# GpSimd takes over the section, relays the half sums and clears the tiles; x is loaded after the first weights; one load for A's output weights

## The chip, the cores and the metric

The kernel runs on one core of a Trainium2 chip. The core has TensorE (PE, matrix products into the accumulation memory PSUM), VectorE (DVE), ScalarE (ACT), GpSimd (POOL) and SyncE (SP), which here issues nearly all DMA transfers. The engines run by themselves and are tied together by semaphores. The metric is the device time of one execution in microseconds (us), and the median over executions is compared.

## What is computed

Two independent decode steps of attention, A and B, each for one query token, 32 heads with 128 elements each, and a cache of 16384 keys; their outputs stand side by side:

```
q = (x @ wq).reshape(1, 1, 32, 128)
scores = einsum("bhqd,bhkd->bhqk", q, k) * 128 ** -0.5
o = einsum("bhqk,bhkd->bhqd", softmax(scores), v)
out = o.reshape(1, 1, 4096) @ wo
return concatenate([a, b], axis=-1)
```

A reads all 16384 keys and values of every head, B only the last 4096. x has 512 elements, wq is 512x4096 and wo 4096x512, all in bf16. Every key, value and weight is used once, so the work is to bring 352 MB into the core and to do little with each byte.

## The kernel before

The program is written out by hand, one function for each engine; no scheduler changes the order. Inside one section (`tc.tile_critical`, L498) the five engines run freely. The section has an owner, `sync_engine=SP`: at the entry all engines wait for a signal of the owner, and at the end the owner gathers the others.

**Loads.** A is worked in 16 loads of two heads, B in 4 loads of eight heads; each is 8 MB of keys and 8 MB of values (`loads`, `st.R` heads at a time, for B in two halves `u`). SP (`_sync_program`, L126 and on) issues, all on one hardware queue: the query weights of A and of B (4 MB each, L132, into the tile `vt`), keys of load 0, then in turn keys of load i and values of load i-1 (L150), and at the end the output weights, cut into pieces (L171): A's in two of 2 MB, B's in five of 2, 1, 0.5, 0.25 and 0.25 MB. Keys have two buffers (`kt`), values one (`vt`). SP waits before keys of load i until the reduction of load i-2 is done (`s_red`), before values of load i-1 until the product with the values of load i-2 is done (`s_pv`), and before keys of load 1 until the query of A and B is projected (`s_q`). The pieces of the output weights wait for the product of the last load but one.

**Start.** GpSimd writes ones and makes from them an identity and a placement matrix (L180 to L189). ScalarE issues the loads of the two x rows (L199, 1 KB each) before anything else. VectorE clears what has to be zero: the tiles for the spread x (`xb_flat`), the selection tiles `sel`, two accumulators, and a 64-column strip `zero` (L245 to L249), and then makes masks and offsets out of the identity (L253 to L264). TensorE turns x into columns (`xT`), VectorE copies them spread out into `xb` (L271), and TensorE multiplies with the query weights when they are there: 32 matmuls of 512 columns for A, 32 for B.

**A load.** VectorE multiplies keys with the query (`mult`, L292) and adds the upper half of the 128 products to the lower half (`add`, L300). TensorE adds up the 64 half sums to 8 by matmuls with the identity (`red`). VectorE adds the last 8 (`scores`, L306), ScalarE takes the exponential (L216), TensorE multiplies with the values (`pv`), and VectorE picks the diagonal (`pick`, L320 to L327), which TensorE sums into the tile `f`. `add` is what releases `red`, by the semaphore `s_add`, which counts four quarters of a load (`NB` = 4). Load 0 is worked in four parts and load 1 in two, so that their adds post one or two quarters each. VectorE's order in load i is `mult(i)`, `scores(i-1)`, `add(i)`, `pick(i-1)`.

**End.** After the last load TensorE turns B's result into columns `oc` (`norm`) and takes the pieces of the output weights in order (`cx.pieces`, L514 and on): 32 matmuls of 512 columns for A, then 64 of 256 columns for B in groups of 32, 16, 8, 4 and 4. Each piece waits for its own semaphore. Every matmul is recorded at L364 (`mm`), so the tiles tell them apart: `red<-vt,ocA` and `red<-vt,ocB` are the output products. VectorE and ScalarE copy the rows out of PSUM and SP stores them (L174).

Of the kernel before, what the change touches and what calls it, by code (L numbers as in the profile page):

```python
# [19 lines left out]
KEYS = 256  # L20
NB = 4
# [153 lines left out]
    cx.s_end.wait(e, 32)  # L175


def _pool_program(nc, cx):
    e = nc.gpsimd
    e.memset(cx.one[:, :], 1.0)  # L180
    e.memset(cx.ones_col[:, :], 1.0)
    cx.s_own.on(e.memset(cx.ones, 1.0))
    cx.s_own.wait(e, 1)
    cx.s_pool.on(e.affine_select(
        out=cx.ident[:, :], in_=cx.ones[:, 0:P], pattern=[[-1, P]], compare_op=ALU.is_equal,
        fill=0.0, base=0, channel_multiplier=1,
    ))
    w = cx.place_at + 2 * P
    cx.s_pool.on(e.affine_select(  # L189
        out=cx.place[:, :], in_=cx.ones[0 : 2 * H, 0:w], pattern=[[1, w]], compare_op=ALU.is_equal,  # L190
        fill=0.0, base=-cx.place_at, channel_multiplier=-cx.n_r,
    ))


def _scalar_program(nc, cx, loads):
    e = nc.scalar
    stA, stB = cx.sts
    for w, st in enumerate(cx.sts):
        st.s_x.on(e.dma_start(out=cx.row[0:1, w * st.D : (w + 1) * st.D], in_=st.x[0, 0:1, :]), 16)  # L199
    n = 0  # L200
    for st in cx.sts:
        m = st.N // st.R // 512
        n += m
        cx.s_q.wait(e, n)
        st.s_qall.on(e.copy(st.qall[:, :], cx.red[:, 0:m, :].rearrange("p j f -> p (j f)")))
    cx.s_dve.wait(e, cx.n_off)
    for i, st in enumerate(loads):
        if i == stA.L:
            _orow(e, cx, stA)
        cx.s_sc.wait(e, i + 1)  # L210
        j = i if st is stA else i - stA.L
        for u in range(st.U):
            p = _p_view(cx, st, u)
            for g in range(st.R):
                h = st.f_at + (j * st.U + u) * st.R + g
                ins = e.activation(  # L216
                    out=p[:, :, g, :],
                    in_=cx.sc[:, u * st.keys : (u + 1) * st.keys].rearrange("p (t e) -> p t e", e=4),
                    func=ACT.Exp, scale=SCALE, bias=st.off[:, g : g + 1], accum_out=cx.cs[:, h : h + 1],
                )  # L220
            cx.s_p.on(ins)
    _orow(e, cx, stB)
    w = stB.DN // 2
    stB.s_o.wait(e, 1)
    stB.s_row.on(e.copy(cx.row[0:1, stB.at + w : stB.at + 2 * w], cx.out_ps(stB)[1]))
# [10 lines left out]
def _vector_program(nc, cx, loads):  # L236
    e = nc.vector
    stA, stB = cx.sts
    own = cx.s_dve

    def did(ins):
        return own.on(ins)

    for st in cx.sts:
        did(e.memset(st.xb_flat, 0.0))  # L245
        did(e.memset(st.sel[:, :], 0.0))
    for acc in cx.acc:
        cx.n_acc = did(e.memset(acc[:, :], 0.0))
    n = did(e.memset(cx.zero, 0.0))  # L249
    cx.n_zero = n  # L250
    cx.s_pool.wait(e, 1)
    ident = cx.ident[:, :]
    n = did(e.tensor_reduce(out=cx.rows, in_=ident.rearrange("p (c w) -> p w c", w=H), axis=AX.X, op=ALU.add))  # L253
    own.wait(e, n)
    for st in cx.sts:
        rows = cx.rows[:, 0 : 4 * st.R].rearrange("p (g e) -> p g e", e=4)
        did(e.tensor_reduce(out=st.mask[:, :], in_=rows.rearrange("p g e -> p e g"), axis=AX.X, op=ALU.add))
        did(e.tensor_reduce(out=st.sel[:, st.sel_at : st.sel_at + st.R], in_=rows, axis=AX.X, op=ALU.add))
        n = did(e.tensor_reduce(
            out=st.off[:, :], in_=ident.rearrange("p (i g) -> p g i", g=st.R), axis=AX.X, op=ALU.add,  # L260
        ))
    own.wait(e, n)
    for st in cx.sts:
        cx.n_off = did(e.tensor_scalar(  # L264
            out=st.off[:, :], in0=st.off[:, :], scalar1=-1.0, scalar2=1000.0, op0=ALU.add, op1=ALU.mult,
        ))
    for st in cx.sts:
        st.s_xT.wait(e, 1)
        xT = cx.xT(st)
        for g in range(st.R):  # L270
            ins = e.tensor_copy(  # L271
                st.xb[:, :, g, :].rearrange("p c (i r) -> p r c i", r=st.R)[:, g, :, :],
                xT.rearrange("p (c o) -> p c o", o=1).broadcast_to([P, st.KC, P // st.R]),
            )
            if g < st.R - 1:
                did(ins)
        st.s_xb.on(ins)

    def mult(i, k0, k1):
        st = loads[i]  # L280
        j = i if st is stA else i - stA.L
        for u in range(st.U):
            a, b = max(k0, u * st.keys), min(k1, (u + 1) * st.keys)
            if a >= b:
                continue
            if k0 == 0 or st.U > 1:
                sem = cx.s_k[_slot(i)][u]
                sem.seen = sem.seen + 16
                sem.wait(e, sem.seen)
            k = cx.kt[:, _slot(i), a:b, :]  # L290
            q = st.qall[:, (j * st.U + u) * DH : (j * st.U + u + 1) * DH]
            n = did(e.tensor_tensor(  # L292
                out=k, in0=k, in1=q.rearrange("p (o d) -> p o d", o=1).broadcast_to([P, b - a, DH]), op=ALU.mult,
            ))
        return n

    def add(i, k0, k1, n):
        k = cx.kt[:, _slot(i), k0:k1, :]
        own.wait(e, n)
        cx.s_add.on(e.tensor_tensor(  # L300
            out=k[:, :, 0 : DH // 2], in0=k[:, :, 0 : DH // 2], in1=k[:, :, DH // 2 : DH], op=ALU.add,
        ), NB * (k1 - k0) // KEYS)

    def scores(i):
        cx.s_red.wait(e, NB * (i + 1))
        cx.s_sc.on(e.tensor_reduce(  # L306
            out=cx.sc[:, :], in_=cx.red[:, :, :].rearrange("p b (k w) -> p (b k) w", w=W), axis=AX.X, op=ALU.add,
        ))

    pv = 0  # L310

    def pick(i):
        nonlocal pv
        st = loads[i]
        j = i if st is stA else i - stA.L
        for u in range(st.U):
            pv += 1
            cx.s_pv.wait(e, pv)
            at = st.sel_at - (j * st.U + u) * st.R
            did(e.tensor_copy(cx.win[u][:, :], st.sel[:, at : at + H]))  # L320
            acc = cx.acc[u][:, :].rearrange("p (e d) -> p e d", d=DH)
            n = did(e.tensor_tensor(  # L322
                out=acc, in0=acc,
                in1=st.mask[:, :].rearrange("p (x o) -> p x o", o=1).broadcast_to([P, 4, DH]), op=ALU.mult,
            ))
            own.wait(e, n)
            cx.s_pick.on(e.tensor_reduce(  # L327
                out=cx.s[u][:, :], in_=acc.rearrange("p x d -> p d x"), axis=AX.X, op=ALU.add,
            ))

    def norm(st):
        at = st.f_at
        st.s_rows.wait(e, 1)
        st.s_recip.on(e.reciprocal(cx.recip[at : at + H, :], cx.f[at : at + H, DH : DH + 1]))
        st.s_oc.wait(e, 1)
        st.s_ocs.on(e.tensor_copy(st.oc[:, :], cx.oc_out(st)))

    for i, st in enumerate(loads):
        n = KEYS // (4, 2)[i] if i < 2 else KEYS
        if i in (0, stA.L):  # L340
            st.s_qall.wait(e, 1)
        for k in range(0, KEYS, n):
            m = mult(i, k, k + n)
            if i and k == 0:
                scores(i - 1)
            add(i, k, k + n, m)
        if i:
            pick(i - 1)
            if i == stA.L:
                norm(stA)  # L350
    scores(len(loads) - 1)
    pick(len(loads) - 1)
    norm(stB)
    stA.s_o.wait(e, 1)
    stA.s_row.on(e.tensor_copy(cx.row[0:1, 0 : stA.DN], cx.out_ps(stA)[0]))
    stB.s_o.wait(e, 1)
    w = stB.DN // 2
    stB.s_row.on(e.tensor_copy(cx.row[0:1, stB.at : stB.at + w], cx.out_ps(stB)[0]))  # L358


def _tensor_program(nc, cx, loads):
    e = nc.tensor
    stA, stB = cx.sts
    mm = lambda *a, **k: e.matmul(*a, skip_group_check=True, **k)  # L364

    cx.s_pool.wait(e, 2)
    cx.s_dve.wait(e, cx.n_zero)
    mm(cx.f[0 : 2 * H, 0:DH], lhsT=cx.zero[:, 0 : 2 * H], rhs=cx.zero, start=True, stop=True)
    for w, st in enumerate(cx.sts):
        st.s_x.wait(e, 16)  # L370
# [78 lines left out]
    n = len(loads)  # L449
# [20 lines left out]
def kernel(  # L470
# [19 lines left out]
    cx = _Ctx()  # L490
# [4 lines left out]
    cx.sts = (stA, stB)  # L495
    loads = [stA] * stA.L + [stB] * stB.L

    ctx.enter_context(tc.tile_critical(sync_engine=mybir.EngineType.SP))  # L498
    _alloc(nc, cx, ctx, stA, stB)
    sem = lambda name: _Sem(nc, ctx, name)  # L500
    for st in cx.sts:
        for name in ("wq", "x", "xT", "xb", "qall", "rows", "recip", "orow", "oc", "ocs", "o", "row"):
            setattr(st, f"s_{name}", sem(f"{name}{st.name}"))
    for name in ("q", "red", "pv", "own", "pool", "dve", "sc", "p", "add", "pick", "end"):
        setattr(cx, f"s_{name}", sem(name))
    cx.s_k = [[sem(f"k{a}{u}") for u in range(2)] for a in range(2)]
    for pair in cx.s_k:
# [2 lines left out]
    cx.s_v = [sem(f"v{u}") for u in range(2)]  # L510
    cx.s_vlast = [sem(f"vl{u}") for u in range(2)]
    J = stA.J
    cx.pieces = [(stA, 0, J // 2, sem("woA0")), (stA, J // 2, J // 2, sem("woA1"))]
    j0 = 0  # L514
    for x in (J // 2, J // 4, J // 8, J // 16, J // 16):
        cx.pieces.append((stB, j0, x, sem(f"woB{j0}")))
# [40 lines left out]
```

The softmax here doesn't subtract the row's maximum and nothing guards it: scores larger than these inputs give would overflow.

## Time and profile before

| | us |
|---|---|
| median of 4 runs | 822.43 (822.02 to 822.47) |
| the profiled execution | 822.12 |
| its span, first to last instruction | 820.4 |
| PE, DVE, ACT, POOL busy | 339.0, 603.5, 35.5, 1.3 |
| DMA queue of SP, share of the 16 engines' span | 99.3% |
| bytes moved, mean rate | 352.42 MB, 430 GB/s |
| granted TensorE clock, mean | 0.694 of full speed |

The profile is of one execution. Times in its views are counted from the start of the span; 1.7 us of the execution's own time lie outside the span. The busy time of an engine says how long it worked and not whether anyone waited for it; that is in the chain of waits, which is followed back from the last instruction, and in the timeline, where a bracket behind a row names the idle time before it and what ended it. A PE matmul's duration has its pipeline in it: a row of 512-column matmuls shows 0.38 us each at full clock while one starts every 0.21 us.

### The profile page before, as it was taken

Reading aid. Unit: us, or ns where it says so; the run is one execution under the profiler, and the core shown is the slowest. Engines: PE = TensorE matmul, PEld = TensorE weight load, DVE = VectorE, ACT = ScalarE, POOL = GpSimd, SP = SyncE. Lnnn points to the kernel's source line nnn. Section 1 sums busy time; section 2 is a strip of 40 time slices with the busy share of each in tenths; the row PEclk is TensorE's granted clock in tenths of the full one; section 3 lists DMA queues with packets and bytes.
Section 4 is the critical chain, followed back from the end, with each engine's and each line's share of the span. In section 5 each row is a group of like instructions: output and inputs, shape, how many; then the busy total and the mean of one; then the engine's idle time right before and its main releaser. Section 6 shows DMA issues by size and latency. Waiting matters only on the chain. (4 is left out here: it accounts for less than half of the span.)

```text
span 820.4 us, 5948 instructions
## 1 busy us (share of the span) xinstructions
PE 339.0 (41%) x2149; PEld 128.2 (16%) x2149; DVE 603.5 (74%) x172; ACT 35.5 (4%) x134; POOL 1.3 (0%) x9
## 2 busy tenths in 40 slices
PE   3433346152324344351617061524243353715277
PEld 1111112020101111110202020201011121202023
DVE  2089995959595968768595959595959969696912
ACT  0100000000000000000000000000000001010110
POOL 0000000000000000000000000000000000000000
PEclk9867578585868565677667585857675776658579
DMA  9999999999999999999999999999999999999997
GB/s 384 435 457 412 457 412 457 412 457 413 454 415 454 412 457 412 457 412 454 415 454 416 451 419 447 422 447 422 444 425 422 447 416 431 433 435 431 435 431 317
DMA packets 8223, 352.42 MB, mean 430 GB/s; under 512 B 916, under 2 KB 920, under 8 KB 1304
## 3 DMA queue, kind: packets, MB, share of 16 engines
q1 hardware_dynamic: 8212, 352.33, 99.3%
q8 instruction: 4, 0.07, 0.0%
q14 instruction: 3, 0.02, 0.0%
q10 hardware_dynamic: 4, 0.00, 0.0%
HBM read 352.32 MB, written 0.00 MB: 429 GB/s over the span
## 5 line engine op out<-in xcount | busy, mean ns | idle before, releaser
L292 DVE TENSOR_TENSOR kt<-kt,qallA 128x32768 bf16<-128x32768 bf16 (+2 forms) x20 | 276.2, 13810 | 156.1 <-DMA kt<-in_A_k_cache_dram 156.1
L364 PE MATMUL acc<-vt,p 128*8 128x512 bf16 (+1 forms) x1216 | 113.8, 553 | 354.6 <-PEq L42 354.6
L364 PE MATMUL red<-kt,ident 128*128 x640 | 181.4, 451 | 43.4 <-PEq L42 43.3
L300 DVE TENSOR_TENSOR kt<-kt 128x16384 bf16<-128x16384 bf16 (+2 forms) x24 | 174.3, 7262 | 0.2
L364 PEld LDWEIGHTS acc<-vt,p 128*8 128x8 bf16 (+1 forms) x1216 | 37.3, 114 | 429.9 <-issue 422.9
L364 PEld LDWEIGHTS red<-kt,ident 128*128 128x128 bf16 x640 | 71.8, 112 | 149.6 <-issue 103.1
L292 DVE TENSOR_TENSOR kt<-kt,qallB 128x16384 bf16<-128x16384 bf16 x8 | 69.5, 8691 | 14.1 <-DMA kt<-in_B_k_cache_dram 14.1
L306 DVE TENSOR_REDUCE sc<-red 128x256 f32<-128x2048 f32 x20 | 45.7, 2284 | 9.5 <-PE red L364 9.5
L216 ACT ACTIVATE p<-sc,offA 128x256 bf16<-128x256 f32 x32 | 16.0, 500 | 605.0 <-DVE sc L306 605.0
L364 PE MATMUL f<-s,win 128*32 128x128 f32 x48 | 11.5, 329 | 59.4 <-PEq L42 59.4
L364 PE MATMUL red<-vt,kt 128*128 128x512 bf16 x64 | 15.5, 404 | 8.3 <-DMA vt<-in_A_wq_dram 6.3
L216 ACT ACTIVATE p<-sc,offB 128x128 bf16<-128x128 f32 x32 | 12.4, 388 | 116.2 <-DVE sc L306 116.2
L327 DVE TENSOR_REDUCE s<-acc 128x128 f32<-128x512 f32 x24 | 16.6, 692 | 0.8
L364 PEld LDWEIGHTS f<-s,win 128*32 128x32 f32 x48 | 4.4, 124 | 70.3 <-issue 70.1
L322 DVE TENSOR_TENSOR acc<-acc,maskA 128x512 f32<-128x512 f32 x16 | 11.1, 693 | 0.0
L320 DVE COPY win<-selB 128x32 f32<-128x32 f32 x8 | 1.4, 179 | 12.4 <-PE acc L364 12.4
L364 PEld LDWEIGHTS red<-vt,kt 128*128 128x128 bf16 x64 | 6.4, 102 | 17.0 <-issue 10.7
L364 PE MATMUL acc<-kt,p 128*16 128x512 bf16 x64 | 5.3, 505 | 4.3 <-PEq L42 4.3
L364 PE MATMUL red<-vt,ocA 128*1 128x512 bf16 x32 | 7.1, 379 | 0.0
L320 DVE COPY win<-selA 128x32 f32<-128x32 f32 x16 | 2.8, 175 | 5.0 <-PE acc L364 5.0
L216 ACT ACTIVATION_READ_ACCUMULATOR p<-sc,offB 128x1 f32 x32 | 6.0, 187 | 0.0
L216 ACT ACTIVATION_READ_ACCUMULATOR p<-sc,offA 128x1 f32 x32 | 6.0, 187 | 0.0
(47 smaller groups left out, 35.3 us busy)
## 6 DMA issues: line engine op xcount, KB each, us to landing
kt<-in_B_k_cache_dram SPq DMA_DIRECT2D x8, 4096.0 KB, 34.6
vt<-in_B_v_cache_dram SPq DMA_DIRECT2D x6, 4096.0 KB, 29.3
kt<-in_B_v_cache_dram SPq DMA_DIRECT2D x2, 4096.0 KB, 39.5
vt<-in_A_wq_dram SPq DMA_DIRECT2D x1, 4096.0 KB, 12.3
vt<-in_B_wq_dram SPq DMA_DIRECT2D x1, 4096.0 KB, 21.5
vt<-in_A_wo_dram SPq DMA_DIRECT2D x2, 2048.0 KB, 22.7
vt<-in_B_wo_dram SPq DMA_DIRECT2D x1, 2048.0 KB, 29.3
vt<-in_B_wo_dram SPq DMA_DIRECT2D x1, 1024.0 KB, 31.2
```

Source lines behind the costliest of these rows:

```text
L216: ins = e.activation(out=p[:, :, g, :], in_=cx.sc[:, u * st.keys : (u + 1) * st.keys].rearrange("p (t e) -> p t e", e=4), func=ACT.Exp, sc ...
L292: n = did(e.tensor_tensor(out=k, in0=k, in1=q.rearrange("p (o d) -> p o d", o=1).broadcast_to([P, b - a, DH]), op=ALU.mult,))
L300: cx.s_add.on(e.tensor_tensor(out=k[:, :, 0 : DH // 2], in0=k[:, :, 0 : DH // 2], in1=k[:, :, DH // 2 : DH], op=ALU.add,), NB * (k1 - k0) ...
L306: cx.s_sc.on(e.tensor_reduce(out=cx.sc[:, :], in_=cx.red[:, :, :].rearrange("p b (k w) -> p (b k) w", w=W), axis=AX.X, op=ALU.add,))
L320: did(e.tensor_copy(cx.win[u][:, :], st.sel[:, at : at + H]))
L322: n = did(e.tensor_tensor(out=acc, in0=acc, in1=st.mask[:, :].rearrange("p (x o) -> p x o", o=1).broadcast_to([P, 4, DH]), op=ALU.mult,))
L327: cx.s_pick.on(e.tensor_reduce(out=cx.s[u][:, :], in_=acc.rearrange("p x d -> p d x"), axis=AX.X, op=ALU.add,))
L364: mm = lambda *a, **k: e.matmul(*a, skip_group_check=True, **k)
```

## The change

- The section's owner is GpSimd instead of SP.
- `add` no longer signals TensorE. It posts to a new semaphore `s_half`, and GpSimd, which had been idle after the start, waits for each of the 24 posts in turn and adds 1, 2 or 4 to `s_add`.
- The first `add` of a load waits for the end of `scores(i-1)` instead of for the end of its `mult`.
- GpSimd clears `sel`, `xb_flat` and the strip `zero`, after the placement matrix; VectorE keeps the two accumulators. VectorE's first reduction and TensorE's first matmul wait for GpSimd's last clear.
- ScalarE issues the loads of x after GpSimd has made the identity.
- A's output weights come as one load of 4 MB with one semaphore, so that A's 32 output matmuls follow one wait.

```diff
+def _parts(i):
+    return (4, 2)[i] if i < 2 else 1
 ...
 def _pool_program(nc, cx):
     e = nc.gpsimd
+    stA, stB = cx.sts
 ...
+    for st in cx.sts:
+        e.memset(st.sel[:, :], 0.0)
+        e.memset(st.xb_flat, 0.0)
+    cx.s_pool.on(e.memset(cx.zero, 0.0))
+    n = 0
+    for i in range(stA.L + stB.L):
+        m = _parts(i)
+        for _ in range(m):
+            n += 1
+            cx.s_half.wait(e, n)
+            e.sem_inc(cx.s_add.h, NB // m)
 ...
 def _scalar_program(nc, cx, loads):
     e = nc.scalar
     stA, stB = cx.sts
+    cx.s_pool.wait(e, 1)
     for w, st in enumerate(cx.sts):
 ...
 (VectorE)
-    for st in cx.sts:
-        did(e.memset(st.xb_flat, 0.0))
-        did(e.memset(st.sel[:, :], 0.0))
     for acc in cx.acc:
-        cx.n_acc = did(e.memset(acc[:, :], 0.0))
-    n = did(e.memset(cx.zero, 0.0))
-    cx.n_zero = n
-    cx.s_pool.wait(e, 1)
+        did(e.memset(acc[:, :], 0.0))
+    cx.s_pool.wait(e, 3)
 ...
     def add(i, k0, k1, n):
         k = cx.kt[:, _slot(i), k0:k1, :]
-        own.wait(e, n)
-        cx.s_add.on(e.tensor_tensor(
+        if i and k0 == 0:
+            cx.s_sc.wait(e, i)
+        else:
+            own.wait(e, n)
+        cx.s_half.on(e.tensor_tensor(
             out=k[:, :, 0 : DH // 2], in0=k[:, :, 0 : DH // 2], in1=k[:, :, DH // 2 : DH], op=ALU.add,
-        ), NB * (k1 - k0) // KEYS)
+        ))
 ...
 (TensorE)
-    cx.s_pool.wait(e, 2)
-    cx.s_dve.wait(e, cx.n_zero)
+    cx.s_pool.wait(e, 3)
     mm(cx.f[0 : 2 * H, 0:DH], lhsT=cx.zero[:, 0 : 2 * H], rhs=cx.zero, start=True, stop=True)
 ...
-    ctx.enter_context(tc.tile_critical(sync_engine=mybir.EngineType.SP))
+    ctx.enter_context(tc.tile_critical(sync_engine=mybir.EngineType.Pool))
 ...
-    cx.pieces = [(stA, 0, J // 2, sem("woA0")), (stA, J // 2, J // 2, sem("woA1"))]
+    cx.pieces = [(stA, 0, J, sem("woA"))]
```

## The prediction

> **What bounds the kernel now.** I read the DMA lines of the page first, because a kernel that reads every byte once should be bound there.
>
> ```profile
> DMA  9999999999999999999999999999999999999997
> GB/s 384 435 457 412 457 412 457 412 457 413 454 415 454 412 457 412 457 412 454 415 454 416 451 419 447 422 447 422 444 425 422 447 416 431 433 435 431 435 431 317
> ...
> q1 hardware_dynamic: 8212, 352.33, 99.3%
> ```
>
> The 16 engines are busy in every slice but the last, on one queue. At the mean of 430 GB/s an 8 MB transfer (8.39 million bytes) takes 19.5 us and 4 MB 9.75 us. So an edit in the middle counts only if it makes SP issue too late for the queue to stay fed; an edit that touches the first issue, or what comes after the last landing, counts in full. The chain of waits says the same of the end:
>
> ```profile
> 784.83 32.29 DMA vt<-in_B_wo_dram
> ...
> 817.16 0.40 PE red L364 x4
> ...
> 817.59 0.42 DVE row L358
> ```
>
> The last 0.25 MB of B's output weights lands at 817.12, four matmuls and a copy follow, then the store and the exit up to 820.4. Next the timeline of PE before that:
>
> ```profile
> 805.48 0.26 PE L364 MATMUL oc_ps<-orow,place 32*128 32x32 bf16 x4 [0.65 <-ACT orow L231]
> 805.67 6.85 PE L364 MATMUL red<-vt,ocA 128*1 128x512 bf16 x31
> 812.35 0.27 PE L364 MATMUL red<-vt,ocB 128*1 128x256 bf16 x2
> ...
> 812.46 1.80 PE L364 MATMUL red<-vt,ocB 128*1 128x256 bf16 x30
> 814.70 1.04 PE L364 MATMUL red<-vt,ocB 128*1 128x256 bf16 x16 [0.44 <-DMA vt<-in_B_wo_dram]
> 815.92 1.00 PE L364 MATMUL red<-vt,ocB 128*1 128x256 bf16 x12 [0.19 <-DMA vt<-in_B_wo_dram]
> 817.16 0.38 PE L364 MATMUL red<-vt,ocB 128*1 128x256 bf16 x4 [0.24 <-DMA vt<-in_B_wo_dram]
> ```
>
> PE has hardly any room: A's 32 matmuls run without a wait from 805.67 to B's first at 812.35 to 812.46 (one per 0.21 us), and B's groups then wait 0.44, 0.19 and 0.24 us for their pieces. When A's two pieces land is in the output loads' times from issue to landing, asked for the first issue (782.08) and the second (782.45) alone:
>
> ```profile
> DMA to landing us min/median/max: 20.4/20.4/20.4
> ```
>
> ```profile
> DMA to landing us min/median/max: 24.9/24.9/24.9
> ```
>
> So the first half is there at 802.5 and the second at 807.4. The first 16 matmuls, 805.67 to 809.1, cover the second landing.
>
> **The change part by part.**
>
> *A's weights in one load.* It takes away one issue of 0.43 us on SP, which lies beside a queue that is fed for another 20 us: nothing. The bytes and the queue's order are the same, so the 4 MB lands where the second half did, 807.4. But all 32 matmuls now wait for it: PE, ready at 805.67, starts A at 807.41, 1.74 us late. At unchanged speed A is done 6.75 us later, 814.2; B's 32 matmuls take 1.7 us (30 start in 1.53, one per 0.053), to 815.9; the groups of 16, 8 and 4, all landed by then, take 0.85, 0.43 and 0.21, to 817.4, where the last four start instead of 817.16. The three waits have swallowed the rest: +0.25 us.
>
> *The clock in that gap.* PE's speed is not constant; the windows view (us of the window, length, PE busy with its count, other engines, then granted clock) has it:
>
> ```profile
> 320.00:323.40 3.40, 1.37 (x28) 0.38 (x16) 3.40 (x3) 0.00 (x0) 0.00 (x0) 1.00 0.80 347
> 323.40:326.80 3.40, 1.90 (x6) 0.73 (x7) 0.76 (x2) 0.00 (x0) 0.00 (x0) 0.50 1.24 540
> ...
> 203.90:207.30 3.40, 1.48 (x28) 0.49 (x20) 3.40 (x3) 0.00 (x0) 0.00 (x0) 0.99 0.76 328
> ...
> 804.60:808.00 3.40, 2.75 (x19) 1.23 (x18) 0.35 (x2) 0.36 (x1) 0.00 (x0) 1.00 1.01 434
> 808.00:811.40 3.40, 3.40 (x17) 1.34 (x16) 0.00 (x0) 0.00 (x0) 0.00 (x0) 1.00 0.98 417
> ```
>
> The clock is half or full in stretches of 3.41 us: 1.37 us of PE work in a stretch was followed by half clock (1.39 at 678.4 too), 1.48 (203.9) by full (1.00 from 207.3). In the stretch from 804.7 PE works 2.75 us. After the change it keeps 0.25 of small matmuls and 0.7 after 807.41: 0.95 us, well under 1.37. So the stretch from 808.1 to 811.5 runs at half: 8 matmuls in place of 16, 1.71 us late, and as PE is behind the landings by then, all of it is on the end. It is itself full of work, as the stretch from 784.2 was (3.26 us busy, clock 0.50, the next at 1.00), so the next is at full clock.
>
> The edges need not lie there in another execution. PE is idle from 802.93 to 807.41 but for 0.42 us at 804.42 and 0.26 at 805.48, so a stretch that begins anywhere from about 802.1 to 805.1 holds under 1.37 us: nearly nine places in ten give a half stretch. Where it begins at 805.5 to 806.6 it holds too little work to be followed by a full one (about a third of the places), which costs 2.4 to 3.0 us. Bounds of this term: 0 and 3.0; I take 1.71, the case of this trace.
>
> The Trainium skill weighs otherwise: its page "TensorE: Matmul & The Clock Gate", section "Part 1: The HAM clock gate", lets the clock fall after at least one idle window of about 3.4 us. Taken literally a wait of 1.7 us in a window that also has work would leave the clock full, and the end would move by the 0.25 us alone. The rows above, where windows with over a third of work were followed by half, decide for me. The page also says that the window runs freely against the kernel's start, which no single trace here shows.
>
> *The owner.* SP now waits for GpSimd's signal instead of giving it. Its first load goes out at 1.02, after ScalarE's at 0.97 and with GpSimd's first work at 1.01; the exit's signals took SP 0.5 us in two waits, the longest 0.4. Each end may move by up to 0.4 us either way; SP need not signal before it issues, and GpSimd already ends the program, so I take -0.1 at each: -0.2.
>
> *x later.* ScalarE's issue moves from 0.97 behind the identity (done at 1.85), so behind A's query weights (SP, 1.02) and beside B's. A 1 KB load issued into a busy queue is B's row: issued at 1.52, at PE at 6.85, 5.3 us.
>
> ```profile
> 6.86 0.29 PE L364 MATMUL oc_ps<-one,row 1*128 1x1 bf16 x4 [2.07 <-DMA row<-in_B_x_dram]
> 13.45 1.01 PE L364 MATMUL red<-vt,kt 128*128 128x512 bf16 x2 [6.30 <-DMA vt<-in_A_wq_dram]
> ```
>
> From 1.9 that is 7.2 for A's row, and B's behind it between 7.6 and 12.5 (another 5.3). With the steps of 0.3 (PE) and 1.29 (DVE) both are ready by 14.1 at the latest, A's by 8.5; the query weights arrive at 13.45. At worst 0.6 us, and that has its own cover: SP issues keys of load 1 on the query's signal at 31.0, while keys of load 0 arrive at 43.8 (VectorE's first `mult`): 12 us. Taken as 0. Moving x's two issues away from SP's first may also let the first packet go sooner; 0 to 0.5 us (the lengthened first issue on ScalarE), taken as 0.
>
> *Clears on GpSimd.* Its 384-column clear took 0.41 us, the one-column ones 0.10: about 0.82 ns a column above the 0.1. So 1024, 2048, 128 and twice some 62 columns are 0.9, 1.8, 0.2 and 0.3: 3.2 us, or 3.6 in proportion to the 0.41. From 2.2 they end at 5.4 to 5.8, where VectorE's strip was cleared at 4.13. VectorE's masks (1.33 us) end by 7.2, near x. Cover as above; 0.
>
> *Relay.* Each of 24 posts passes through GpSimd. PE started 0.54 us after the first add (50.52 to 51.06), a wake-up with register work; a second hop costs at most that, 13 us if all were exposed. `red` releases keys two loads on, and the tightest is the issue at 74.53, which landed 27.1 us later, 19.5 of it its own: some 7 us of queue ahead. At the end the last add is over at 778.1, while PE is on the values of load 18 until 784.5: covered. 0.
>
> *`add` waits for `scores`.* It loses an overlap of 0.08 us (769.43 against 769.51) per load on VectorE, which idled 170 us for keys: 0.
>
> Sum on the profiled execution: 822.12 + 0.25 + 1.71 - 0.2 = 823.9. Its own time is 0.31 under the median, so 824.2 beside 822.43.
>
> **The rivals.**
> 1. *The clock stays full* (the other side: not slower). The mechanism is the edge of the stretch: if one begins between 805.1 and 805.5, or PE's chain comes late enough to close the gap, A runs at full speed: 822.43 + 0.25 - 0.2 = 822.5. It decides once PE does 1.4 us of work in the stretch around 807. The two rows at 203.9 speak for how near the border is; 0.95 us against it.
> 2. *Two half stretches*: 0.25 + 2.4 to 3.0 - 0.2, so 824.9 to 825.5. For it: PE's chain also gets shorter where the values of load 19 (half clock at 797.8, 0.51) run at full clock, which lengthens the gap.
> 3. *x too late*: if the 1 KB rows wait behind the weights and keys until 43.8, the query (17.6 us from 13.4 to 31.0) ends near 64 and keys of load 1 come 20 us late: 842. B's 5.3 us speak against it.
> 4. *The change doesn't reach the end, and the start gains*: first packet and exit both at their best, -0.9 to -1.7: 820.7 to 821.5.
>
> **How the numbers follow.** About 0.2%, 1.64 us, is what a measurement of this kernel can tell from no change: below 820.8 is faster, above 824.1 slower. One half stretch 0.47, clock full 0.30, two half stretches 0.17, x late 0.02, start gains 0.04. The first lies at 823.5 to 824.5 with the bounds of the owner, about two thirds of it above 824.1; slower is 0.32 + 0.17 + 0.02 = 0.51, faster 0.03, same 0.46. The range takes in the full clock and two half stretches: 822.2 to 825.7.
>
> **What would show it.** In the profile after: A's first output matmul preceded by a wait of about 1.6 us on `vt<-in_A_wo_dram`; a stretch at 0.50 over part of A's 32 matmuls; B's groups without waits, the last four starting near 819 instead of 817.16; PE in the chain of waits at the end; a DMA queue as busy as before and landings at the same times. Wrong would be A's weights landing well before 807, a clock of 1.00 over A, or a DMA line with a gap in it.

## The result

The changed kernel takes 823.44 us (median; 821.97 to 824.89) against 822.42 (822.00 to 822.92): the ratio is 1.0012 with a 95% interval of 1.0007 to 1.0017. It is slower by 1.0 us, which the interval tells from no change, and lies inside the 0.2% that the prediction set as its own line. The median says less than the spread: before, all 52 executions lie within 0.9 us (in a later set of 33, from 822.23 to 823.35); after, 7 of 32 lie from 821.97 to 822.24, one at 822.67, 13 from 823.02 to 823.53 and 11 from 823.83 to 824.89. The profiled execution took 824.49 us and has a span of 822.4, so it belongs to the last group.

The DMA line of the page differs from before in the last slice alone, which is less full because the span goes on after the loads. The queue moved the same bytes, in 144 fewer packets:

```profile
DMA  9999999999999999999999999999999999999996
...
q1 hardware_dynamic: 8068, 352.33, 99.1%
```

The end of the chain of waits (start, us, what) has changed. B's last piece is no longer in it; A's load and, behind it, TensorE are:

```profile
781.32 25.75 DMA vt<-in_A_wo_dram
...
807.20 12.46 PE red L379 x92
...
819.69 0.42 DVE row L373
```

A's 4 MB lands at 807.07, and from there TensorE works without a break to the end. The timeline of PE shows the wait and what follows:

```profile
803.22 0.26 PE L379 MATMUL oc_ps<-orow,place 32*128 32x32 bf16 x4 [0.65 <-ACT orow L248]
807.20 9.16 PE L379 MATMUL red<-vt,ocA 128*1 128x512 bf16 x29 [3.72 <-DMA vt<-in_A_wo_dram]
815.99 0.38 PE L379 MATMUL red<-vt,ocB 128*1 128x256 bf16 x4
...
816.64 3.01 PE L379 MATMUL red<-vt,ocB 128*1 128x256 bf16 x52
```

In this execution TensorE was ready at 803.5, 2.2 us sooner than in the profile before, and waited 3.72 us. A's matmuls then took over 9 us in place of 6.9, and B's run on without a wait, because their pieces had all landed by 816.9. The windows view (us, length, PE busy, other engines, granted clock, DMA) says why A's took so long:

```profile
799.20:802.60 3.40, 1.88 (x30) 1.00 (x22) 2.04 (x4) 0.00 (x0) 0.00 (x0) 1.00 0.89 386
802.60:806.00 3.40, 0.26 (x4) 0.16 (x4) 0.35 (x2) 0.36 (x1) 0.00 (x0) 0.99 0.99 424
806.00:809.40 3.40, 2.20 (x6) 0.73 (x7) 0.00 (x0) 0.00 (x0) 0.00 (x0) 0.50 1.01 434
809.40:812.80 3.40, 3.40 (x10) 0.99 (x9) 0.00 (x0) 0.00 (x0) 0.00 (x0) 0.50 0.93 386
812.80:816.20 3.40, 3.40 (x21) 1.39 (x22) 0.00 (x0) 0.00 (x0) 0.00 (x0) 1.00 0.73 289
```

In the stretch from 802.6 PE had 0.26 us of work; the next ran at half clock, and as it held only 2.20 us, so did the one after it. So 5.6 us of A's matmuls ran at half clock. This is the prediction's case of two half stretches.

### The profile page after: what moved, and what is told of

Same layout as the page of the kernel before. It is cut to its first block, busy times and chain, and to the rows that moved or that the text cites. A ratio compares the mean times of both kernels' runs of the same rounds, so it can differ in the third digit from the quotient of the medians.

```text
span 822.4 us, 5952 instructions
## 1 busy us (share of the span) xinstructions
PE 342.1 (42%) x2149; PEld 129.2 (16%) x2149; DVE 603.8 (73%) x167; ACT 35.5 (4%) x134; POOL 4.3 (1%) x14
## 5 line engine op out<-in xcount | busy, mean ns | idle before, releaser
L379 PE MATMUL red<-kt,ident 128*128 x640 | 183.4, 457 | 43.2 <-PEq L42 43.2
L379 PE MATMUL red<-vt,ocA 128*1 128x512 bf16 x32 | 9.8, 481 | 3.7 <-DMA vt<-in_A_wo_dram 3.7
```

## The experiments

**One edit makes the whole of it.** The first run takes that edit back from the changed kernel, the second makes it alone in the kernel before.

```diff
-    cx.pieces = [(stA, 0, J, sem("woA"))]
+    cx.pieces = [(stA, 0, J // 2, sem("woA0")), (stA, J // 2, J // 2, sem("woA1"))]
```

> The changed kernel with A's output weights in two loads of 2 MB again; all else as changed. Theory 'gap and clock' (PE waits for the whole of A's weights, and the clock falls in that gap): 822.0 to 822.4 us, every execution within 0.6 us of the next as before the change, A's first output matmul at 803 to 806 without a wait for weights. Rival 'relay and start' (the added time comes from GpSimd's relay, x or the clears): stays near 823.4. Rival 'transfer' (one load of 4 MB lands later than two of 2 MB): as the first.

Measured: 822.23 us (822.05 to 822.46 in 11 executions), beside 822.49 (822.23 to 823.35) for the kernel before on the same chip; ratio 0.9995 (0.9986 to 1.0004). The added time and the spread are gone with this edit alone, while the relay, the owner, the clears and the later x remain. The profile has one thing more to teach. Its windows, and then its timeline:

```profile
801.40:804.80 3.40, 1.50 (x22) 0.79 (x14) 1.64 (x4) 0.17 (x1) 0.00 (x0) 1.00 0.99 419
804.80:808.20 3.40, 3.15 (x11) 1.04 (x12) 0.19 (x1) 0.19 (x1) 0.00 (x0) 0.50 1.06 453
```

```profile
805.26 7.86 PE L379 MATMUL red<-vt,ocA 128*1 128x512 bf16 x29
...
815.84 1.01 PE L379 MATMUL red<-vt,ocB 128*1 128x256 bf16 x12 [0.27 <-DMA vt<-in_B_wo_dram]
817.06 0.38 PE L379 MATMUL red<-vt,ocB 128*1 128x256 bf16 x4 [0.21 <-DMA vt<-in_B_wo_dram]
```

A half stretch came here too, over A's first matmuls. It cost nothing: A had begun at 805.26, 1.9 us before A's second half landed at 807.21, and by the last pieces PE was waiting for weights again. So the head start that the first half of A's weights gave also hid the clock here.

The other way round, the kernel before with the one edit:

```diff
-    cx.pieces = [(stA, 0, J // 2, sem("woA0")), (stA, J // 2, J // 2, sem("woA1"))]
+    cx.pieces = [(stA, 0, J, sem("woA"))]
```

> The kernel before with one edit: A's output weights in one load of 4 MB. Theory 'gap and clock': 823.4 to 824.4 us, executions spread over 2 us and more. Rival 'relay and start': 822.4 as before.

Measured: 823.68 us (822.35 to 824.76), beside 822.49; ratio 1.0015 (1.0006 to 1.0024). The one edit makes the whole of the loss and of the spread. Its profiled execution was one of the undisturbed ones (822.35), and so shows what the wait costs without the clock. Its windows and its timeline:

```profile
805.60:809.00 3.40, 1.87 (x12) 0.86 (x13) 0.28 (x2) 0.36 (x1) 0.00 (x0) 1.00 0.99 424
809.00:812.40 3.40, 3.40 (x18) 1.30 (x16) 0.00 (x0) 0.00 (x0) 0.00 (x0) 1.00 0.96 407
```

```profile
807.39 6.42 PE L364 MATMUL red<-vt,ocA 128*1 128x512 bf16 x29 [0.99 <-DMA vt<-in_A_wo_dram]
813.44 0.38 PE L364 MATMUL red<-vt,ocB 128*1 128x256 bf16 x4
...
814.09 2.79 PE L364 MATMUL red<-vt,ocB 128*1 128x256 bf16 x48
817.09 0.38 PE L364 MATMUL red<-vt,ocB 128*1 128x256 bf16 x4 [0.21 <-DMA vt<-in_B_wo_dram]
```

A starts as late as in the changed kernel, and yet B's last group still waits 0.21 us for its weights. At full clock the late start alone costs nothing.

**Is it the wait or the larger transfer?** The changed kernel with two loads again, but a wait for both ahead of A's first matmul:

```diff
+        if st is stA and j0 == 0:
+            cx.pieces[1][3].wait(e, 16)
         sem.wait(e, 16)
```

> The changed kernel with A's output weights in two loads of 2 MB, but TensorE waits for both before its first matmul of A. Theory 'gap and clock': as the changed kernel, 823.0 to 824.4 us with a spread of 2 us. Rival 'transfer': 822.0 to 822.4, as with two loads.

Measured: 823.87 us (822.13 to 824.66), beside 822.49; ratio 1.0012 (1.0003 to 1.0022). That is as long as the changed kernel takes. The transfer falls as a cause: what counts is that no matmul of A may start on the first half.

**Is it the wait or the clock?** The changed kernel, with matmuls into an accumulator that nobody reads any more, so that PE has work in the gap. They add work that the computation doesn't need.

```diff
     norm(stB)
+    for t in range(7):
+        mm(cx.acc[0][:, :], lhsT=cx.ident[:, :], rhs=cx.kt[:, _slot(n - 2), 4 * t : 4 * t + 4, :], start=True, stop=True)
```

> The changed kernel with seven more matmuls of 512 columns (1.5 us at full clock, into an accumulator that nobody reads any more) between B's last small matmuls and the wait for A's weights. The wait stays, the gap is shorter. Theory 'gap and clock': the granted clock over A's matmuls is 1.00, 822.0 to 822.6 us and a spread under 1 us. If the wait itself and not the clock costs the time: 823.4 as the changed kernel.

Measured: 822.26 us (822.03 to 823.31), beside 822.49; ratio 0.9998 (0.9989 to 1.0007). A starts no sooner and the loss is gone from the median. Two of the 11 executions still took 823.02 and 823.31, so the spread of 1.28 us is over the 1 us expected; neither was profiled, and the kernel before has three such among its 33 on the same chip (823.07 to 823.35). The timeline (one of the seven matmuls has no record in it) and the windows of its profile:

```profile
805.88 1.46 PE L379 MATMUL acc<-kt,ident 128*128 128x512 bf16 x6 [0.16 <-issue]
807.38 6.42 PE L379 MATMUL red<-vt,ocA 128*1 128x512 bf16 x29
```

```profile
804.80:808.20 3.40, 2.55 (x15) 1.13 (x16) 0.35 (x2) 0.36 (x1) 0.00 (x0) 1.00 0.97 414
808.20:811.60 3.40, 3.40 (x17) 1.34 (x16) 0.00 (x0) 0.00 (x0) 0.00 (x0) 1.00 0.96 407
```

With 2.55 us of work in the stretch the next is at full clock. With three such matmuls in place of seven:

> As the kernel with seven matmuls in the gap, but with three (0.64 us at full clock). If what decides is how much TensorE work a stretch of 3.41 us holds, three are too few where the gap is 3.7 us and enough where it is 1.7 us: between the changed kernel and the one with seven, a median of 822.4 to 823.3 us, with single executions above 824. If any matmul in the gap is enough: 822.2 to 822.4, no execution above 823.4.

Measured: 823.40 us (822.33 to 824.75), beside 822.49; ratio 1.0013 (1.0004 to 1.0022): as if none were there. The median expected was a little lower. The pair shows that it is not enough to have some work in the gap: seven matmuls do it and three do not. The profiled execution is the fastest one (822.33): TensorE was ready only at 806.4, the stretch from 805.7 held 2.60 us of work, and the clock over A was 1.00.

**How much a stretch costs.** Three more profiled executions of the changed kernel.

> The changed kernel once more, for a second profile. Theory 'gap and clock': the time of the profiled execution goes with how much of A's 32 output matmuls lies in stretches at half clock, half of that time being lost: none of it near 822.2 us, one stretch near 823.5, two near 824.5.

> The changed kernel, one more profiled execution, to see the clock of the middle group of its times (823.0 to 823.5 us). Theory 'gap and clock': one stretch at half clock over the first part of A's output matmuls, 2.2 to 2.8 us of it beside them; if the execution falls into another group, none (822.2) or two stretches (824.5).

> The same once more: its time goes with the length of half clock beside A's 32 output matmuls, half of that length being lost.

They took 825.14, 823.89 and 823.66 us (the first stands in a set of five executions, 822.02 to 825.14). None fell into the group from 823.0 to 823.5, and none was without half clock. The last has one half stretch beside A:

```profile
805.20:808.60 3.40, 1.53 (x11) 0.69 (x11) 0.35 (x2) 0.36 (x1) 0.00 (x0) 1.00 0.94 405
808.60:812.00 3.40, 3.40 (x9) 0.98 (x8) 0.00 (x0) 0.00 (x0) 0.00 (x0) 0.51 0.99 419
812.10:815.50 3.40, 3.40 (x26) 1.48 (x27) 0.00 (x0) 0.00 (x0) 0.00 (x0) 1.00 0.87 351
```

All profiles in which A waits for its whole weights follow. "Half clock beside A" is how much of the time from A's first matmul to the end of its last lies in stretches at half clock; the last column is how long after the landing of B's last piece the last output matmul started:

| execution | its time | A starts | half clock beside A | last landing | last matmul | after it |
|---|---|---|---|---|---|---|
| one load alone | 822.35 | 807.39 | 0 | 817.05 | 817.20 | 0.15 |
| seven in the gap | 822.35 | 807.38 | 0 | 817.09 | 817.24 | 0.15 |
| three in the gap | 822.33 | 807.36 | 0 | 817.07 | 817.22 | 0.15 |
| changed, third look | 823.66 | 807.33 | 3.41 | 817.04 | 818.45 | 1.41 |
| changed, second look | 823.89 | 807.20 | 4.34 | 816.87 | 818.76 | 1.89 |
| wait for both | 824.58 | 807.32 | 5.52 | 817.03 | 819.46 | 2.43 |
| changed | 824.49 | 807.20 | 5.59 | 816.90 | 819.38 | 2.48 |
| changed, again | 825.14 | 807.66 | 5.80 | 817.36 | 819.94 | 2.58 |

Half of the half-clock time is 1.71, 2.17, 2.76, 2.79 and 2.90 us; the last column is below that by 0.28 to 0.33 us in every row. As 0.15 us pass after the landing in any case, the delay itself is below it by 0.43 to 0.48 us. The clock accounts for the delay, less some 0.4 us of room that PE has before it. The room is in the profile of one load alone too: the last matmul ahead of the final four starts at 816.61, and the final four wait for their weights until 817.09.

**The rest of the change, part by part.** Each is set on the kernel before. The executions of the kernel before have between 1.67 and 2.2 us outside their span, so spans are compared as well. The first edit is the owner:

```diff
-    ctx.enter_context(tc.tile_critical(sync_engine=mybir.EngineType.SP))
+    ctx.enter_context(tc.tile_critical(sync_engine=mybir.EngineType.Pool))
```

> The kernel before with one edit: GpSimd owns the section. If the owner gives the 0.2 to 0.3 us that the changed kernel with two loads gains on the kernel before: 822.1 to 822.3 us, SP's first load at 0.96 in place of 1.02. If not: 822.45.

Measured: 821.89 us (821.71 to 822.40), below the expected 822.1 to 822.3, beside 822.47 (822.07 to 822.72); ratio 0.9994 (0.9985 to 1.0003). The spans' medians are 820.2 and 820.4; the other 0.4 us lie outside the span (1.68 to 1.76 in this kernel's executions, a median of 2.07 in those before, which begin at 1.67). What sets that was not found, and it is not put down to the edit: the changed kernel, with the same owner, has 2.06 to 2.25. The first issue on SP in the timeline stands at 0.96, where it was 1.02:

```profile
0.96 0.42 SPq L132 DMA_DIRECT2D vt<-in_A_wq_dram  x1
```

From the end of the wait for the last store to the end of the span it is 1.11 us (1.26 before). The gain in the span is about 0.2 us, 0.06 of it at the start and 0.15 at the end. The interval of the ratio reaches past 1, so the gain rests on the spans and on these two places.

The second run has x behind the identity and the clears on GpSimd, with SP as owner, without a relay and with two loads:

> The kernel before with x loaded behind GpSimd's identity and the clears of the selection tiles, the spread x and the strip on GpSimd; SP owns the section, no relay, two loads. As the prediction has it, hidden: 822.3 to 822.5 us. If x's two issues had held back SP's first packet: 822.0 to 822.2. If the later query cost anything: above 822.7, and a gap in the DMA line.

Measured: 822.47 us (822.37 to 822.75), beside 822.47; ratio 1.0001 (0.9992 to 1.0010), spans 820.4 and 820.4. This part is hidden. The third is the relay, with its wait of the first add for the scores:

```diff
+    n = 0
+    for i in range(cx.sts[0].L + cx.sts[1].L):
+        m = _parts(i)
+        for _ in range(m):
+            n += 1
+            cx.s_half.wait(e, n)
+            e.sem_inc(cx.s_add.h, NB // m)
...
-        own.wait(e, n)
-        cx.s_add.on(e.tensor_tensor(
+        if i and k0 == 0:
+            cx.s_sc.wait(e, i)
+        else:
+            own.wait(e, n)
+        cx.s_half.on(e.tensor_tensor(
```

> The kernel before with the half sums posted to GpSimd, which relays them to TensorE, and the first add of a load waiting for the scores; nothing else. As the prediction has it, covered by the queue: 822.3 to 822.5 us, with TensorE's first reduction at most 0.5 us later after the first add. If the relay reaches the end: 823 and more.

Measured: 822.42 us (822.23 to 822.74), beside 822.47; ratio 1.0000 (0.9991 to 1.0009), spans 820.3 and 820.4. TensorE's first reduction starts 0.61 us after the first add, as in the changed kernel, where it was 0.54. This part is hidden too.

So the changed kernel with A's weights in two loads has a median 1.2 us under that of the changed kernel and 0.26 under that of the kernel before; for the latter the interval does not exclude no difference.

## Why the prediction was right, and where it was off

**The bound.** This was right. No part that lies beside the queue (relay, x, clears, the later first add) shows in any time, and the whole loss is at the end, where the prediction had put it.

**The start.** It is hidden, as the prediction had it. Timeline of PE in the changed kernel:

```profile
8.14 0.29 PE L379 MATMUL oc_ps<-one,row 1*128 1x1 bf16 x4 [2.58 <-DMA row<-in_A_x_dram]
10.61 0.29 PE L379 MATMUL oc_ps<-one,row 1*128 1x1 bf16 x4 [2.18 <-DMA row<-in_B_x_dram]
13.30 3.14 PE L379 MATMUL red<-vt,kt 128*128 128x512 bf16 x7 [2.40 <-DMA vt<-in_A_wq_dram]
```

A's row came at 8.1, 0.9 us later than the 7.2 worked out, and B's at 10.6 (7.6 to 12.5), both before A's query weights. SP issued keys of load 1 at 31.6 in place of 31.0, against 12 us of cover. GpSimd's clears ended at 5.20, a little before the 5.4 to 5.8 worked out. After the first add TensorE started 0.61 us later, where it was 0.54; the bound was a second 0.54.

**The owner.** The prediction took -0.2 from within bounds of 0.4 at each end, and -0.2 was measured in the span.

**The wait for A's weights.** The start at 807.41 was right (807.20 in the profile, 807.39 alone). The +0.25 us that should follow at full clock is wrong: the undisturbed execution of the kernel with the one edit has no such delay. The step that failed is "At unchanged speed A is done 6.75 us later, 814.2; B's 32 matmuls take 1.7 us". B's do not wait for A's to be done. In that execution B's first start at 813.44, A's last starts at 814.08, 0.64 us later, and twelve of B's matmuls start in between. With that the chain has some 0.4 us of room where the sum had a debt of 0.25: together about the 0.64. In the profile before, B's first two started at 812.35, 0.13 us after their weights had landed at 812.22, and so could not show how far the two groups overlap.

**The clock.** The mechanism is right, and shown: taken away by matmuls in the gap, brought back by one edit on the kernel before. The rule of the Trainium skill that was set against the rows ("TensorE: Matmul & The Clock Gate", "Part 1: The HAM clock gate": the clock falls after at least one idle window) would have kept the clock full and left the prediction's 0.25 us alone. Here stretches with 1.19 to 1.56 us of work in 3.4 were followed by half clock, or stayed at it, so the rows decided rightly. The same page's statement that the window runs freely against the kernel's start agrees with the four profiles of the changed kernel: counted from the start of the span, their stretches begin at 802.6, 803.2, 804.7 and 805.2.

The term itself was 1.71 for the likeliest case, with 2.4 to 3.0 for two stretches. One stretch puts the last matmul 1.4 us behind the last landing where it was 0.15 without: 1.3 us. Two put it 1.7 to 2.4 us later than without. The times follow: 823.66 for one where 824.2 was forecast, 823.9 to 825.1 for two where 824.9 to 825.5 was, 822.35 for none (seven in the gap, with the same owner) where 822.5 was. All the cases came, and each 0.2 to 1.0 us below its price: the 0.25 was not there, the 0.4 of room was, and the second stretch can lie partly in the gap. The median is in the group from 823.0 to 823.5. No profile fell into that group itself; the nearest, 823.66, has one half stretch, the likeliest case of the prediction. The undisturbed group's spans of 819.9 to 820.1 us and the 1.3 us of one stretch make 821.2 to 821.4, where the spans of the middle group are 820.9 to 821.4. That the group is this case is argued from that, not shown. So is the count that follows from it: 7 of 32 executions without half clock, where the prediction's count of places left one in ten and its chance was 0.30.

**Chances.** Slower by over 0.2% had 0.51 and the measured 0.12% falls on the other side of that line. It was a forecast of 1.76 us against a line at 1.64, so the debt that was not there and the room that was decided it. The share of two thirds above 824.1 within the likeliest case had no working behind it.

## What to carry to other kernels

Where a kernel is bound by its loads, look at how the last stage is let in: here splitting a load cost an issue of 0.43 us that nobody waited for, and let work start on the first half. The wait of TensorE, 1.0 to 3.9 us long, was not priced by its length alone, but by the work that the clock's stretch around it still held: it cost between nothing and 2.4 us. Seven matmuls that nobody needs were worth 1.2 us. When one kernel's executions fall into groups, a single profile shows one of them, and it takes several to find the mechanism.

## What was not expected of the hardware

- The border of the clock is not where one pair of rows put it, and it is not one amount of work. In the profile before 1.48 us of PE work in a stretch was followed by full clock and 1.37 to 1.39 by half. At the end of the program 1.50 (two loads), 1.53 (third look) were followed by half, and 1.87 (one load alone) and 1.88 (changed) by full. Elsewhere in these profiles a stretch with 1.40 us was followed by full (owner alone, from 435.9) and one with 1.81 by half (changed, from 669.4). What decides between 1.4 and 1.8 us is open.
- Matmuls with one output row in different rows of PSUM overlap: B's first start 0.64 us before A's last, though they come after it in the program. (Their weights had landed at 812.10.) It was not tried what sets this.
- The time outside the span differs by up to 0.5 us between executions of one kernel (1.67 to 2.2 us before the change). For effects of some 0.2 us the spans say more here than the times.
